# A convolution and two-layer kernel: new homes for w2's parts, block sums in place, another order at the end of layer 1, transposes in rows of four

## The chip, the cores and the metric

One Trainium2 chip, one core. The metric is the device time of one execution in microseconds (us), the median of three runs. Five engines work from queues of their own and wait for each other by semaphores: TensorE (PE; its weight loads PEld), VectorE (DVE), ScalarE (ACT), GpSimd (POOL) and SyncE (SP), which here issues nearly all DMAs.

## The reference

```python
def reference(A_q, A_k, A_v, A_shift_k, A_ssm_k, A_ssm_D, B_x, B_w1, B_b1, B_w2, B_b2, c, w_mod):
    # S = 2048 tokens, D = 640 channels, F = 1728 hidden; all fp32
    x = A_q
    mod = (_silu(c) @ w_mod).reshape(c.shape[0], 6, 1, -1)
    sa, ca, ga, sb, cb, gb = (mod[:, i] for i in range(6))
    h = _layernorm(x, axis=-1) * (1 + ca) + sa
    # _A_ref: 4-tap causal conv of k, times v; a long causal conv per channel (FFT); times h
    x = x + ga * _A_ref(h, A_k, A_v, A_shift_k, A_ssm_k, A_ssm_D)
    h = _layernorm(x, axis=-1) * (1 + cb) + sb
    r = relu(h @ w1 + b1)                 # layer 1
    return x + gb * ((r * r) @ w2 + b2)   # layer 2
```

## The kernel before, in words

**Stages.** The long convolution runs block by block (five blocks of 128 channels) as two-step transforms on TensorE (keys `pa`, `h`, `x`, `qp`, `t`, `y`), with the gate and the first residual (`fin`). The result x1 goes to DRAM; its first two chunks of 256 tokens stay on the chip in the buffers X1a and X1b. Then comes the dense part.

**Layer 1** works in four passes of 512 tokens, two halves T1 and T2 of 256. w1 lies transformed on the chip: six pairs of 128-column blocks (`w16_0` to `w16_5`, in the tiles `TAGS` = S1, S0, S3, S2, S5, S4), and two leftover blocks (12 and 13, the last with 64 columns) in `s6`. Every number is split in a high and a low part (`split`: a copy on ScalarE, a subtraction on VectorE), and each product is three matmuls of 256 columns (`l1`). Passes 1 to 3 use a 2 x 2 block product with seven instead of eight multiplications (`pair`); the seventh is done later (`late`). The leftovers have plain products (`rest`, 25 matmuls a half). Between passes `tokens` loads, normalises and transposes the next chunk (`turned`: two transposes and one evicting, scaling operation for each of five blocks). Hidden tiles are squared and stored in DRAM (`h_d`).

**Layer 2** works in eight chunks of 256 tokens. `w2_pair(p)` loads two raw tiles of w2 into the ring of four staging tiles STG0 to STG3, splits three blocks, forms four sums on GpSimd in a scratch half of `xf`, and splits these as well: six blocks into the tile of the same pair of w1 (`TAGS[p]`), the seventh into `extra2[p]` (two to each of X1a and X1b, the last two in `s6`). `w2_last` puts leftover blocks into `s6`. Hidden tiles come back from DRAM through a ring of eight quarters UP0.0 to UP1.3 (`h_pair`, `h_last`), which the tiles of layer 1 use as well, in the order in which the program asks for them; VectorE forms four sums, and both engines split them into `xp1r`, `ka`, `kz` or `xa`. A chunk has 146 products of 320 columns in seven PSUM banks (`second_layer`), then sums, the gate row, the residual (`xres`, halves of `xf`) and the output.

**Order.** The program records a graph of operations and orders it itself (`order`): a list scheduler that takes, for each engine, the ready operation with the highest priority out of the table `URGE` (due times, in tenths of us, negative), with a cost for each, a model of the DMA queue, and costs `ENTER` and `LEAVE` where TensorE changes its `form`. The order it finds is fixed in the program (`keep_order`); each engine works in it strictly. SyncE has at most six transfers under way (`OUT`): a later one waits for the landing of the sixth before it. All operations are recorded at one line (L407), so rows of the trace are told apart by their tiles.

## Time and profile before

| | us |
|---|---|
| median of three runs (lowest, highest) | 658.59 (658.23, 659.29) |
| the profiled execution | 658.96 |
| its span, first to last instruction | 657.2 |
| TensorE busy in it | 629.6 (96%) |
| VectorE, ScalarE, GpSimd busy | 516.1, 358.1, 226.8 |

```profile
PEclk8999999999999999999999999999999999999999
DMA  9898989999896722563756632145555443553353
```

These two lines of the page cut the span in 40 slices: TensorE's granted clock and the busy share of the 16 DMA engines, both in tenths. The convolution reaches to about 265 us, layer 1 from 280 to 479, layer 2 from 472 to 652. TensorE is the engine that is busy nearly throughout, so a time is read from where it stands still and from what it waited for.

### The profile page before, as it was taken

The page shows a single profiled execution, that of the slowest core. Times are in us where ns is not written, and L with a number is a line of the kernel's source. Part 1 is how long each engine was busy: PE and PEld are TensorE (multiplying, and loading weights), DVE is VectorE, ACT ScalarE, POOL GpSimd, SP SyncE. Part 2 cuts the span into 40 slices and gives each one's busy share as a digit, 9 for nine tenths or more (in the row PEclk, how much of TensorE's full clock was granted, in tenths as well). Part 3 has the DMA queues.
Part 4 walks back from the last instruction along what each step waited for, and adds up shares of the span by engine and source line. Part 5 has one row for each costly group of instructions (what it writes and reads, how often), then busy time and mean ns, then how long its engine had stood idle before and what let it go on. Part 6 is the DMA issues. An engine that isn't in the chain of part 4 may idle for free.

```text
span 657.2 us, 17277 instructions
## 1 busy us (share of the span) xinstructions
PE 629.6 (96%) x7012; PEld 584.4 (89%) x7012; DVE 516.1 (79%) x969; ACT 358.1 (54%) x681; POOL 226.8 (35%) x294
## 2 busy tenths in 40 slices
PE   7999999999999999899999999999989999999996
PEld 7888779878878878499999999999978999999996
DVE  1758848699978666886886787778899989788896
ACT  3554767885866775556585664456463424233321
POOL 1528649768786756311324200235400000000000
PEclk8999999999999999999999999999999999999999
DMA  9898989999896722563756632145555443553353
GB/s 223 217 272 284 267 231 249 208 234 216 229 241 164 142 56 72 156 208 89 213 152 194 193 112 75 56 140 166 159 147 171 151 137 118 166 176 120 114 157 81
DMA packets 143464, 111.00 MB, mean 169 GB/s; under 512 B 50836, under 2 KB 123348, under 8 KB 143384
## 3 DMA queue, kind: packets, MB, share of 16 engines
q1 hardware_dynamic: 141252, 109.28, 60.1%
q8 instruction: 55, 0.90, 0.6%
q10 hardware_dynamic: 2068, 0.61, 0.4%
q14 instruction: 25, 0.20, 0.1%
q0 software_dynamic: 64, 0.01, 0.0%
HBM read 79.99 MB, written 29.88 MB: 167 GB/s over the span
## 4 chain that ended last, share of the span: by engine, by line
PE 49%; DVE 3%; DMA 2%; ACT 1%; issue 1%; DVEq 0%; ACTq 0%
PE ps L407 49%; DMA up<-h_d 2%; DVE up L407 1%; DMA x<-x_d 1%; DVE w L407 0%; DVE ka L407 0%; DVE s L407 0%; DVE xp1r L407 0%; DVE kz L407 0%; ACT w L407 0%; ACT xf L407 0%; DVE xa L407 0%; DVE outs L407 0%; ACT kz L407 0%; ACT xa L407 0%
## 5 line engine op out<-in xcount | busy, mean ns | idle before, releaser
L407 PE MATMUL ps<-a,gb 128*64 128x128 f32 x1260 | 76.8, 275 | 3.3 <-ACT a L407 2.1
L407 PEld LDWEIGHTS ps<-a,gb 128*64 128x64 f32 x1260 | 69.3, 137 | 11.6 <-ACT a L407 5.4
L407 ACT ACTIVATE up<-ps,b1t 128x256 f32<-128x256 f32 (+1 forms) x112 | 50.6, 471 | 48.4 <-PE ps L407 46.4
L407 PE MATMUL ps<-t,w 128*128 128x256 f32 x504 | 72.7, 284 | 0.3 <-DVE up L407 0.3
L407 PEld LDWEIGHTS ps<-cst,p 64*64 64x64 f32 (+1 forms) x1792 | 60.7, 137 | 11.4 <-issue 6.1
L407 PE MATMUL ps<-cst,p 64*64 64x64 f32 (+1 forms) x1792 | 66.7, 247 | 3.9 <-POOL p L407 2.5
L407 PEld LDWEIGHTS ps<-t,w 128*128 128x128 f32 x504 | 64.8, 189 | 0.7 <-DVE up L407 0.5
L407 ACT ACTIVATE a<-ps 128x512 f32<-128x512 f32 x72 | 40.8, 620 | 31.9 <-PE ps L407 31.8
L407 DVE SCALAR_TENSOR_TENSOR up<-up 128x512 f32<-128x512 f32 (+2 forms) x70 | 45.3, 655 | 11.3 <-ACT up L407 10.6
L407 DVE TENSOR_TENSOR up<-up 128x256 f32<-128x256 f32 (+2 forms) x124 | 44.7, 383 | 7.4 <-DMA up<-h_d 5.7
L407 PE MATMUL ps<-xa,w 128*128 128x256 f32 x342 | 49.5, 284 | 0.0
L407 POOL TENSOR_TENSOR wm<-wm,wm 128x640 f32<-128x640 f32 x24 | 38.2, 1591 | 19.7 <-ACT wm L407 19.1
L407 PEld LDWEIGHTS ps<-xa,w 128*128 128x128 f32 x342 | 44.1, 190 | 0.4 <-DVE xa L407 0.2
L407 PE MATMUL ps<-w,xp1r 128*128 128x320 f32 x216 | 40.1, 310 | 1.9 <-ACT up L407 1.1
L407 PE MATMUL ps<-w,xa 128*128 128x320 f32 x216 | 41.1, 309 | 0.0
L407 PE MATMUL ps<-w,kz 128*128 128x320 f32 x216 | 39.9, 310 | 0.6 <-DVE kz L407 0.6
L407 PE MATMUL ps<-w,ka 128*128 128x320 f32 x216 | 40.4, 309 | 0.0
L407 DVE SCALAR_TENSOR_TENSOR kva<-ps,tap,kva 128x511 f32<-128x511 f32 (+2 forms) x48 | 35.8, 747 | 5.5 <-ACT kva L407 3.8
L407 DVE TENSOR_TENSOR up<-ps,up 128x256 f32<-128x256 f32 (+2 forms) x67 | 28.5, 435 | 13.4 <-PE ps L407 8.3
L407 PEld LDWEIGHTS ps<-w,xp1r 128*128 128x128 f32 x216 | 33.7, 188 | 2.6 <-ACT up L407 1.3
L407 PEld LDWEIGHTS ps<-w,kz 128*128 128x128 f32 x216 | 33.6, 188 | 1.0 <-DVE kz L407 1.0
L407 ACT ACTIVATE kz<-up 128x896 fp32r<-128x896 f32 (+2 forms) x24 | 16.8, 699 | 32.1 <-DVE up L407 31.8
(199 smaller groups left out, 1533.4 us busy)
## 6 DMA issues: line engine op xcount, KB each, us to landing
h_d<-up SPq DMA_DIRECT2D x51, 256.0 KB, 2.5
up<-h_d SPq DMA_DIRECT2D x48, 256.0 KB, 3.5
wm<-in_w_mod_dram SPq DMA_DIRECT2D x30, 320.0 KB, 5.2
w1s<-in_B_w_dram SPq DMA_DIRECT2D x25, 320.0 KB, 3.7
p<-in_A_ssm_k_dram SPq DMA_DIRECT2D x20, 256.0 KB, 4.4
p<-kv_d SPq DMA_DIRECT2D x20, 256.0 KB, 4.6
xp<-in_A_q_dram SPq DMA_DIRECT2D x10, 512.0 KB, 8.0
xf<-x_d SPq DMA_DIRECT2D x8, 640.0 KB, 4.1
```

The lines of the kernel that those rows point to most:

```text
L407: fn(*real, **{k: a.real() if isinstance(a, View) else a for k, a in kw.items()})
```

## The change

1. *Homes.* w2's pair 0 goes into X1a, X1b (four of its six blocks) and the last third of `s6` (two); pairs 1 to 5 into the tile of the w1 pair before their own (`TAGS[p - 1]`). The seventh blocks of pairs 0 to 3 go into `xf`'s place, those of pairs 4 and 5 and both leftover blocks into S4. The residual's tiles move from `xf` to the staging tiles.
2. *Sums in place.* The four sums of a pair overwrite the raw tiles.
3. *Last pass of layer 1.* The late product of the last pair and `h_pair(0, 1)` come ahead of the leftovers, `h_pair(0, 2)` between their halves.
4. *Transposes* of chunks 1 to 7 in rows of four (two blocks in one bank), and in the dense part the form of a TensorE operation is its type: going to an fp32 one is charged 0.04 us, to an fp32r one 0.085.
5. *End of layer 2.* Residual loads and stores by 128 tokens; in the last chunk each block is gated and added as soon as it is there, the block (1, 1) in two parts.
6. *`URGE`* is a new table throughout.

```diff
-ENTER = {(64, 128): 0.104}
-LEAVE = {(64, 64): 0.11}
+ENTER = {(64, 128): 0.104, 4: 0.04, 2: 0.085}
+LEAVE = {(64, 64): 0.11, 4: 0.0, 2: 0.0}
...
     def turn(o, x, hold=()):
-        ..., form=(P, P))
+        ..., form=(P, P) if len(g.nodes) <= g.mlp else 4)
...
-    def turned(n, xh, b):
+    def turned(n, xh, bs):
         g.key = ("xt", n)
-        t = psum(f"xtp_{n}_{b}", (P, 2, P), ...)
-        for i in range(2):
-            with g.as_one(0.11):
-                turn(t[:, i], xh[i][:, b * P : (b + 1) * P])
+        t = psum(f"xtp_{n}_{bs[0]}", (P, len(bs), 2, P), ...)
+        turns = [(j, i) for i in range(2) for j in range(len(bs))]
+        for k in range(0, len(turns), len(turns) if n else 1):
+            some = turns[k:] if n else turns[k : k + 1]
+            with g.as_one(0.11 * len(some)):
+                for j, i in some:
+                    turn(t[:, j, i], xh[i][:, bs[j] * P : (bs[j] + 1) * P])
...
-            for b in range(NB):
-                turned(n, xh, b)
+            for bs in ((0, 1), (2, 3), (4,)) if n else ((b,) for b in range(NB)):
+                turned(n, xh, bs)
...
+        if s == NS - 1:
+            late[0]()
+            h_pair(0, 1)
         r = [out_tile(f, s) for f in (NF - 2, NF - 1)]
         rest(s, 1, [v[:, CH:] for v in r])
         if s == NS - 1:
-            h_pair(0, 1)
-        late[0]()
+            h_pair(0, 2)
+        else:
+            late[0]()
...
-        w = W2S[p] = sbuf(f"w2_{p}", (P, 3840), [whole(TAGS[p])], dtype=F32R)...
-        e = W2X[p] = extra2[p].rearrange("p (a f) -> p a f", a=2)
-        temp = xf[:, 1280 * (p % 2) : 1280 * (p % 2) + 1280]
-        t = temp.rearrange("p (k f) -> p k f", k=4)
+        if p:
+            w = sbuf(f"w2_{p}", (P, 3840), [whole(TAGS[p - 1])], dtype=F32R)...
+            u, v, w = w[:, :, 0:2], w[:, :, 2:4], w[:, :, 4:6]
+        else:
+            u, v = (sbuf(f"w2_0{i}", (P, 1280), [whole(f"X1{i}")], dtype=F32R)... for i in "ab")
+            w = s6[:, 2560:3840].rearrange("p (a k f) -> p a k f", a=2, k=2)
...
         split(w[:, 0, 0], w[:, 1, 0], a[:, 0])
-        split(w[:, 0, 1:3], w[:, 1, 1:3], c)
+        split(u[:, 0], u[:, 1], c)
         g.key = ("w2c", p)
-        sub(pool, t[:, 0], a[:, 1], a[:, 0])
-        sub(pool, t[:, 1], c[:, 1], t[:, 0])
-        sub(pool, t[:, 2], c[:, 1], a[:, 1])
-        sub(pool, t[:, 3], c[:, 0], t[:, 1])
+        sub(pool, a[:, 0], a[:, 1], a[:, 0])
+        sub(pool, a[:, 1], c[:, 1], a[:, 1])
+        sub(pool, c[:, 1], c[:, 1], a[:, 0])
+        sub(pool, c[:, 0], c[:, 0], c[:, 1])
...
-                rows = x1_d.buf.real[n * CH : (n + 1) * CH, :].rearrange("(l p) d -> p l d", p=P)
-                sp_dma(x, in_dram(x1_d, rows, n * CH, n * CH + CH, 31), 2560)
+                for i in range(2):
+                    r0 = n * CH + i * P
+                    sp_dma(x[i], in_dram(x1_d, x1_d.buf.real[r0 : r0 + P, :], r0, r0 + P, 31), 2560)
...
-        for i, k in ((1, 0), (0, 0), (0, 1), (1, 1)):
+        def gated(i, k, t, done=True):
             o = slice(320 * k, 320 * k + 320)
-            mul(dve, c[:, i, k], c[:, i, k], row0b[:, o])
-            add(dve, x[:, i, o], x[:, i, o], c[:, i, k])
-            for a in range(2):
-                (act_dma if a else sp_dma)(osrc[a, :, 2 * n + i, o], x[64 * a : 64 * a + 64, i, o], 1280)
+            mul(dve, c[:, i, k], t, row0b[:, o])
+            add(dve, x[i][:, o], x[i][:, o], c[:, i, k])
+            for a in range(2) if done else ():
+                (act_dma if a else sp_dma)(osrc[a, :, 2 * n + i, o], x[i][64 * a : 64 * a + 64, o], 1280)
+
+        gated(1, 0, c[:, 1, 0])
+        add(dve, c[:, 0, 0], ps7[4], u3)
+        gated(0, 0, c[:, 0, 0])
+        add(dve, u2, ps7[5], u2)
+        gated(1, 1, u2, False)
+        add(dve, c[:, 0, 1], ps7[5], u3)
+        gated(0, 1, c[:, 0, 1])
+        gated(1, 1, ps7[3])
...
-        ("hat", 0): [-1183, -2159],
+        ("hat", 0): [2077, -147],
-        ("xs", 0): [-2103, -1773, -2350, -2609, -2958, -2800, -2077, -2273, -2097, -2777],
+        ("xs", 0): [2417, 665, -2623, -2890, -2813, -1174, 2418, -2946, 2420, 667],
-        ("y", 4): [-2576, -2524, -1940, -2560],
+        ("y", 4): [-937, -770, -770, 587],
-        ("lw1", 0): [-2600, -3062],
+        ("lw1", 0): [-1493, -3444],
...
-    xz = [sbuf(f"xz_{i}", (P, 1280), [whole(f"X1{'ab'[i]}")], dtype=F32R) for i in range(2)]
-    extra2 = [xz[p // 2][:, 640 * (p % 2) : ...] for p in range(4)] + [s6[:, 640 * i : 640 * i + 640] for i in range(2)]
+    xe = sbuf("xe", (P, 2560), [WXB], dtype=F32R)
+    extra2 = [xe[:, 640 * i : 640 * i + 640] for i in range(4)]
     for p in range(NP):
+        if p == 4:
+            se = sbuf("se", (P, 3840), [whole(TAGS[5])], dtype=F32R)
+            extra2 += [se[:, 640 * i : 640 * i + 640] for i in range(2)]
         w2_pair(p)
-    w2_last(NF - 2, s6[:, 1280:2560])
-    w2_last(NF - 1, s6[:, 2560:3840])
+    w2_last(NF - 2, se[:, 1280:2560])
+    w2_last(NF - 1, se[:, 2560:3840])
...
-    xres = [xf[:, 1280 * k : 1280 * k + 1280].rearrange("p (i d) -> p i d", i=2) for k in (1, 0)]
+    xres = [[sbuf(f"xr_{k}_{i}", (P, D), [whole(f"STG{2 * k + i}")]) for i in range(2)] for k in range(2)]
```

## Rows read from the trace of the kernel before

**Rows 1.** Sums by stretch: busy us (operations) by engine, clock, DMA share, GB/s.

```profile
0.00:250.00 250.00, 237.25 (x3958) 203.81 (x3960) 182.06 (x318) 163.48 (x313) 160.23 (x230) 0.99 0.86 215
250.00:284.00 34.00, 29.29 (x314) 22.03 (x314) 26.97 (x48) 18.14 (x33) 14.83 (x15) 1.00 0.41 113
284.00:470.00 186.00, 184.62 (x1531) 181.96 (x1531) 146.67 (x308) 111.12 (x240) 46.94 (x46) 1.00 0.46 144
470.00:500.00 30.00, 26.28 (x180) 24.95 (x179) 25.76 (x54) 14.21 (x26) 4.80 (x4) 1.00 0.60 180
500.00:652.00 152.00, 152.00 (x1038) 151.68 (x1036) 133.04 (x240) 51.17 (x71) 0.00 (x0) 1.00 0.45 138
```

**Rows 2.** Order of time, TensorE: start, us, operation xcount [idle before <-releaser].

```profile
478.29 0.71 PE L407 MATMUL ps<-w,xp1r 128*128 128x320 f32 x3 [0.80 <-DVE up L407]
...
480.42 0.71 PE L407 MATMUL ps<-w,xp1r 128*128 128x320 f32 x3 [1.07 <-ACT up L407]
...
485.10 1.74 PE L407 MATMUL ps<-w,kz 128*128 128x320 f32 x10 [0.57 <-DVE kz L407]
...
499.05 0.41 PE L407 MATMUL ps<-s,kz 128*128 128x320 f32 x1 [1.23 <-DVE kz L407]
```

**Rows 3.** Order of time, VectorE, where layer 2 begins.

```profile
476.02 1.89 DVE L407 TENSOR_TENSOR up<-up 128x128 f32<-128x128 f32 x4 [2.26 <-DMA up<-h_d]
477.83 0.41 DVE L407 TENSOR_TENSOR up<-ps,up 64x256 f32<-64x256 f32 x1
...
497.53 0.89 DVE L407 TENSOR_TENSOR up<-up 128x256 f32<-128x256 f32 x2 [1.05 <-DMA up<-h_d]
498.44 0.55 DVE L407 TENSOR_TENSOR kz<-up,kz 64x384 fp32r<-64x384 f32 x1
```

**Rows 4.** Order of time, VectorE, its last three operations.

```profile
652.16 0.49 DVE L407 TENSOR_TENSOR outs<-ps,outs 128x320 f32<-128x320 f32 x1
652.68 0.49 DVE L407 TENSOR_TENSOR outs<-outs,gbrow 128x320 f32<-128x320 f32 x1
653.21 0.49 DVE L407 TENSOR_TENSOR xf<-xf,outs 128x320 f32<-128x320 f32 x1
```

**Rows 5.** Order of time, TensorE, transposes (ident,x) among products of layer 1.

```profile
395.26 0.27 PE L407 MATMUL ps<-ident,x 128*128 128x128 f32 x1
395.28 0.60 PE L407 MATMUL ps<-xa,w 128*128 128x256 f32 x3
395.72 0.53 PE L407 MATMUL ps<-kz,w 128*128 128x256 f32 x3
396.08 0.52 PE L407 MATMUL ps<-xa,kz 128*128 128x256 f32 x3
...
408.60 0.60 PE L407 MATMUL ps<-ident,x 128*128 128x128 f32 x4
408.96 0.95 PE L407 MATMUL ps<-t,w 128*128 128x256 f32 x6
409.75 0.53 PE L407 MATMUL ps<-ident,x 128*128 128x128 f32 x3
```

**Rows 6.** Order of time, TensorE and then VectorE, where the convolution ends.

```profile
266.92 1.50 PE L407 MATMUL ps<-ident,q 128*128 128x128 f32 x12 [1.81 <-DVE q L407]
...
277.17 0.93 DVE L407 TENSOR_TENSOR w<-w1s,w 128x640 fp32r<-128x640 f32 x1
278.16 0.99 DVE L407 TENSOR_SCALAR xf<-ps,cbs 128x256 f32<-128x256 f32 x2
```

**Rows 7.** Order of time, GpSimd, two sums of w2's blocks.

```profile
472.28 2.22 POOL L407 TENSOR_TENSOR xf<-w2s,w2s 128x320 f32<-128x320 f32 x1 [9.35 <-DMA w2s<-in_B_w_dram]
474.46 0.87 POOL L407 TENSOR_TENSOR xf<-w2s 128x320 f32<-128x320 f32 x1
```

**Rows 8.** Layer 2: SyncE's waits (us in total, times, longest); its transfers (KB each, us to landing).

```profile
SPq L618 <- DMA out_dram<-xf: 19.3, 6, 3.7
...
xf<-x_d SPq DMA_DIRECT2D x7, 640.0 KB, 4.1
```

More of the change, by code (lines that the diff above doesn't have):

```diff
@@ L681, in mm @@
         ins = [x for x in (a, b) if isinstance(x, View)]
-        g.add("PE", 0.0, (nc.tensor.matmul, "matmul", (o, a, b), dict(start=start, stop=stop, **({"skip_group_check": True} if more else {}))), [o], ins, entries=n, hold=hold, form=(a.p[1] - a.p[0] if isinstance(a, View) else a.shape[0], o.p[1] - o.p[0]))
+        g.add("PE", 0.0, (nc.tensor.matmul, "matmul", (o, a, b), dict(start=start, stop=stop, **({"skip_group_check": True} if more else {}))), [o], ins, entries=n, hold=hold, form=(a.p[1] - a.p[0] if isinstance(a, View) else a.shape[0], o.p[1] - o.p[0]) if len(g.nodes) <= g.mlp else n)
     def turn(o, x, hold=()):
-        g.add("PE", 0.0, (nc.tensor.transpose, "transpose", (o, x, ident), {}), [o], [x] if isinstance(x, View) else [], entries=2, hold=hold, form=(P, P))
+        g.add("PE", 0.0, (nc.tensor.transpose, "transpose", (o, x, ident), {}), [o], [x] if isinstance(x, View) else [], entries=2, hold=hold, form=(P, P) if len(g.nodes) <= g.mlp else 4)
     def copy(eng, o, i, hold=()):
@@ L1522, in l2, with rest2 @@
                 mm(acc, h[a], w[y], first and i == 0, last and i == 2)
+    def rest2(n, ps7, i):
+        k, o = {2: (1, 0), 4: (0, 0), 5: (0, 1), 3: (2, 1)}[i]
+        g.key = ("l2", n)
+        a, c = HS[n, "a"], HS[n, "c"]
+        wa, wc = W2S[NF - 2], W2S[NF - 1]
+        o = slice(320 * o, 320 * o + 320)
+        l2(ps7[i], parts(a, k), (wa[:, 0, o], wa[:, 1, o]), False, False)
+        with g.as_one(0.294):
+            mm(ps7[i], c[:, k], wc[:, 0, o], False, False)
+            mm(ps7[i], cone[n % 2][:, k], wc[:, 1, o], False, False)
     def second_layer(n):
@@ L1528, in second_layer @@
         for p in range(NP):
-            if n == 0 and p + 2 < NP:
+            if n == 0 and 0 < p and p + 2 < NP:
                 h_pair(0, p + 2)
@@ new lines, in ssm_mlp_kernel @@
+        ("h", 3): [-1650, -1932, -1912, -1941, -1635, -1982, -1830, -1874, -1946, -2062, -1893, -2088, -1664, -1905,
+            -1536, -1979],
+        ("h", 4): [-2363, -2396, -2195, -2416, -2436, -2288, -459, -2287, -2054, -1960, -2502, -2144, -2492, -2510,
+            -2065, -1950],
+        ("hat", 0): [2077, -147],
+        ("hat", 1): [-2764, -3073],
+        ("hat", 2): [-2895, -2820],
+        ("hat", 3): [-3432, -2566],
+        ("hat", 4): [-2234, -2234],
+        ("hat", 5): [-2360, -2274],
@@ new lines, in ssm_mlp_kernel @@
+        ("mul", 4): [-2426, -2315, -2426, -2456, -2512, -2158, -2475, -2097, -2331, -2511, -2504, -2503, -2503, -2576,
+            1546, 1259],
+        ("one", 0): [-4261, -4758, -4820, -4274, -4503, -4204],
+        ("out", 0): [-4087, -4801, -5167, -3753, -5132, -5099, -1316, -4223, -5482, -5526, -4965, -5172, -5446, -4631,
+            -5208, -5311],
+        ("out", 1): [-5638, -5177, -5371, -5536, -5347, -5037, -5345, -5486, -5253, -5586, -5462, -5483, -5986, -5687,
+            -5654, -5654],
```

243 lines of the change are left out of this document (111 added, 132 removed), and 655 rows, old and new, of the table URGE.

## The prediction

> **What bounds the kernel now.** I read the sums by stretch first [rows 1]. TensorE is busy for 152.00 of the 152.00 us of layer 2 behind 500 us and for 184.62 of 186.00 us of layer 1; no edit here takes products away, so these two stretches can't give more than 1.4 us together. Its idle time lies in three places: 12.75 us (250.00 - 237.25) in the first 250 us, 4.71 us where the convolution ends and layer 1 begins (250 to 284 us), and 3.72 us where layer 1 ends and layer 2 begins (470 to 500 us). After the last matmul come VectorE's last adds and the last writes, 5.2 us.
>
> Then the order of time in the third place [rows 2]: four gaps, 0.80, 1.07, 0.57 and 1.23 us, together 3.67. For what stands behind them I read VectorE's queue there [rows 3]. At 476.02 it begins work on a hidden tile whose load from DRAM has just landed, after 2.26 us of idling; the bias add that frees a PSUM bank stands behind it and runs at 477.83, and TensorE goes on at 478.29. At 497.53 the same again: 1.05 us for a load that chunk 1 needs, and behind it at 498.44 a small split that chunk 0 needs at once; TensorE waits 1.23 us. So these gaps aren't a lack of VectorE time (25.76 of 30.00 us busy [rows 1]); they are an order in which work that is not yet fed stands ahead of work that is awaited.
>
> **The change, part by part.** The time comes out of the order, so each part is priced by the idle time that it can remove.
>
> *Homes of w2's parts, and the leftover tiles last in pass 3.* No instruction is added: each pair keeps five splits (ScalarE copy, VectorE subtraction) and four GpSimd subtractions. What moves is when they may run. Pair 0 goes into the x1 buffers and a part of `s6` that layer 1 doesn't use; pairs 1 to 5 take the tile of the pair of w1 before their own, so each can be written one pair of layer 1 earlier. `xf` becomes the home of four of the "extra" blocks, and the tile of w1's last pair that of the rest. With pair 5 finished before the leftover products, that tile falls free while two times 25 products are still to run, and the second pair of chunk 0's hidden tiles is asked for ahead of both leftover blocks and the third between them, instead of the second between and the third behind. The work that stood at VectorE's head at 476.02 is thereby earlier in the ring of eight quarters, and its load can be issued earlier. The leftovers' own evictions, two per token half, are now the last ones, so the wait for a bank can recur there: I keep one of 0.7 us, near the 0.57 and 0.80 us of [rows 2]. Term: 3.7 - 0.7 = 3.0 us less. Bounds: all 3.7 us gone, or one wait of the largest size added to all that is there (+1.2).
>
> *Block sums in place.* As many GpSimd operations as before; 0.87 us each when alone and 2.22 us at worst [rows 7]. New are waits: the first sum may start only when both halves of the split of `a[:, 0]` have read it, and the raw tiles are held until the last split, not until the last sum. Behind GpSimd's head stands only the next sum; on SyncE's queue the load of the raw tiles two pairs on. The cover is the pair that is one home ahead. Off the path: 0; bounds 0 and +2.2, one slow sum on it. The operation of 2.22 us ran beside VectorE, the one of 0.87 us hardly [rows 7]. The Trainium skill says of this ("SBUF — State Buffer", section "SBUF: two separate sides") that GpSimd and a VectorE operation with two SBUF inputs exclude each other on a shared port pair for the whole instruction. By that rule in-place sums, which now alternate with VectorE's subtractions, would run nearer to 2.22 than to 0.87 us; four per pair stay behind the products all the same, and the sum is left as it is.
>
> *Transposes in rows of four.* Chunks 1 to 7 of layer 1 have 70 transposes, in 30 runs of one to four now and in 21 rows afterwards. A lone one: from 395.26 to 395.72 us one transpose and three products took 0.46 us; three products alone (395.72 to 396.08) 0.36; the transpose cost 0.10. In a row of four: 408.60 to 409.75 is 1.15 us for four transposes and six products; less 6 x 0.12 leaves 0.43, or 0.108 each [rows 5]. So a row saves nothing that can be seen, though the planner's table now charges 0.04 + 0.085 us for going there and back. Taken: 0. Bound: 9 fewer runs x 0.125 = 1.1 us less; nothing on the other side, since a bank held by two blocks is awaited only by the next chunk's work.
>
> *The last chunk's end.* Before, three VectorE operations follow the last product in line, from 652.16 to 653.70 us, each some 0.52 from start to start [rows 4]. Now each gated block is added as soon as it is there, and for the last one the part without `ps7[3]` has been multiplied and added already: a multiply out of PSUM and an add are left. Term: 0.5 us less. It costs one more multiply and add earlier, beside TensorE. Bounds: 1.0 us more where these two push the last pair back; 0.5 less.
>
> *Residual and output in halves.* Per chunk one more load, two more stores, on SyncE, which has at most six transfers under way. Layer 2 has no TensorE idling to show for SyncE's waits so far [rows 1, 8]. Taken: 0; the other end is the third rival.
>
> *All due times drawn anew.* This is the widest part. Where the convolution ends there is one chain (transform, gate, statistics, normalise, transpose, first products), and other work stands in it on VectorE: a split of w1 of 0.93 us at 277.17 runs ahead of the two evictions (278.16) that the first products of layer 1 wait for, and TensorE waits 1.81 us at 266.92 for a copy that VectorE was late with [rows 6]. In the new table the keys that feed that chain (`hat` 0, the first of `xs` 0, `y` 4) come far forward, and w1's loads come earlier, so its splits can run before the chain. Of 4.71 us I take a third, 1.5. Bounds: 3.7 less (1 us is left), 1.5 more (three splits like that of 0.93 us in the way instead of one, partly covered). For the first 250 us, where the due times of the first blocks hardly change, 0, with 1 us either way.
>
> **Sum.** 3.0 + 0.5 + 1.5 = 5.0 us less. The profiled execution took 658.96 us in all, with a span of 657.2 and 1.8 around it; it would become 654.0. The median of the runs, 658.59, is 0.4 below that execution, so 653.6 us.
>
> **The rivals.**
> First, *both seams close*: boundary 3.7, start 3.7, end 0.5: 7.9 us less, 650.7 us. For it speaks that most of the waits there are waits in a queue and not for a busy engine; against it, that the start is a chain with fixed latencies, of which the rows show one split of 0.93 us and one late copy only.
> Second, *the waits move*: the loads of the hidden tiles land later than planned as they did at 476 and 497 us, and VectorE again stands for them with an eviction behind; the start is as before. Only the end is left: 658.1 us. For it: the order is fixed beforehand, and in both head waits [rows 3] VectorE had come to its work before the load had landed. Against it: the loads are now asked for ahead of the leftovers.
> Third, on the other side, *SyncE's queue in layer 2*. It already waited 19.3 us in six waits for landings of the output, up to 3.7 us each, and a 640 KB residual load takes 4.1 us to land [rows 8]. With 14 transfers a chunk instead of 11 on one queue with six under way, the loads of the next chunk's hidden tiles stand behind stores that wait for VectorE. From the point where they land later than the previous chunk's last product, each of the seven chunk starts shows a gap such as the one of 1.23 us [rows 2]: 8.6 us, less the 5.0 above: 662.2 us. Against it: not one gap in 152 us of layer 2 so far. On halves: the 640 KB load took 4.1 us [rows 8]; the Trainium skill ("DMA: Bandwidth & Descriptors", section "Bandwidth") wants transfers in pieces of a megabyte or more, since each pays a fixed part. By that rule two halves would cost more than the whole and this rival gains; no run here shows a half.
>
> **How the numbers follow.** The forecast has 0.55, both seams 0.15, the waits that move 0.17, SyncE's queue 0.13. About 0.2%, 1.3 us, is what a measurement of this kernel can tell from no change. Faster by more than that: 0.70; within it: 0.17; slower: 0.13. The forecast's own bounds are 1.5 to 2.5 us either way. The range reaches from 649.5 (the first rival with the 1.1 us of the transposes) to 659.2 (the second with 1 us lost in the first 250); outside lie the third and a little on both sides.
>
> **What would show it.** Right: 470 to 500 us (some 2 us earlier by then) with under 1 us of TensorE idling, no eviction behind a wait for a load on VectorE, two VectorE operations behind the last product. The start: under 3.5 us of idling between the last transform and steady layer 1. Transposes: the same 0.11 us each in rows. Wrong: gaps of TensorE at the starts of layer 2's chunks, released by splits that waited for loads; or idling in the first 250 us above 13.8 us; or the four gaps again at other places with the same sum.

## The result, and the profile after

The changed kernel takes 662.52 us (median of 13 runs, 658.28 to 665.11) against 660.16 for the kernel before on the same chip (13 runs): a ratio of 1.0045, 95% interval 1.0024 to 1.0065. It is slower by about 0.45%, where 653.6 us and a gain were predicted; 662.5 also lies above the range. The profiled execution took 664.42 us with a span of 662.6, and the granted clock of TensorE averaged 0.992 in it (before: 0.997).

Each run lists its span and its mean granted clock. (1 - clock) x span is the time that half speed took away, if TensorE had work all the while. Over the 82 runs of the kernel before that were made beside the experiments (on three chips) it is 2.0 us on average and the rest of the time 657.5; over 25 runs of the changed kernel (13 here, 12 in the first experiment) 4.0 and 658.5, with standard errors of 0.2 to 0.4. So of 3.0 us some 2.0 go with the clock and 1.0 with work and waits.

Sums by stretch, as in [rows 1] (busy us (operations) of PE, PEld, DVE, ACT, POOL, then clock, DMA share, GB/s):

```profile
0.00:250.00 250.00, 232.40 (x3892) 201.45 (x3894) 174.69 (x314) 161.74 (x311) 154.97 (x226) 0.99 0.83 212
250.00:284.00 34.00, 30.75 (x367) 24.05 (x364) 26.62 (x47) 17.36 (x32) 15.30 (x17) 1.00 0.33 94
284.00:470.00 186.00, 184.43 (x1520) 181.36 (x1519) 146.05 (x307) 108.84 (x240) 46.24 (x48) 1.00 0.49 150
470.00:500.00 30.00, 26.79 (x168) 25.29 (x168) 26.66 (x55) 16.11 (x28) 5.79 (x5) 0.89 0.51 162
500.00:652.00 152.00, 151.88 (x1035) 151.56 (x1034) 130.40 (x237) 51.66 (x73) 0.00 (x0) 1.00 0.49 141
```

From 470 to 500 us TensorE still stands still for 3.21 us (30.00 - 26.79; 3.72 before), and its clock there is 0.89 instead of 1.00. Behind 500 us nothing has changed. TensorE there, in order of time, answering [rows 2]:

```profile
473.94 0.97 PE L407 MATMUL ps<-xa,w 128*128 128x256 f32 x6 [0.38 <-ACT up L407]
...
486.64 0.41 PE L407 MATMUL ps<-w,kz 128*128 128x320 f32 x1 [0.23 <-DVE kz L407]
...
491.55 0.58 PE L407 MATMUL ps<-xe,xa 128*128 128x320 f32 x2 [1.86 <-ACT xa L407]
492.68 0.63 PE L407 MATMUL ps<-xe,xa 128*128 128x320 f32 x1 [0.55 <-DVE xa L407]
493.11 5.00 PE L407 MATMUL ps<-w,xa 128*128 128x320 f32 x18
```

The four gaps of before are gone, but with one more of 0.19 us these add up to 3.21: the largest is now a wait for the split of a hidden tile of chunk 0 (`xa`). The 18 products behind it take 5.00 us; at full speed the same 18 take 2.79 (shown below). VectorE and ScalarE ahead of that wait, answering [rows 3]:

```profile
478.56 1.15 DVE L407 TENSOR_TENSOR up<-up 128x128 f32<-128x128 f32 x4 [1.30 <-DMA up<-h_d]
...
481.50 0.46 DVE L407 TENSOR_TENSOR up<-up 128x128 f32<-128x128 f32 x1 [0.87 <-DMA up<-h_d]
...
491.53 1.09 DVE L407 TENSOR_TENSOR xa<-up,xa 128x896 fp32r<-128x896 f32 x1
```

```profile
488.81 0.74 ACT L407 ACTIVATE se<-w2s 128x640 fp32r<-128x640 f32 x1 [3.35 <-DMA w2s<-in_B_w_dram]
490.55 0.95 ACT L407 ACTIVATE xa<-up 128x896 fp32r<-128x896 f32 x1 [1.00 <-DVE up L407]
```

VectorE still idles for loads of hidden tiles, 1.30 and 0.87 us. An eviction still stands behind the first of these loads (480.23 us), but TensorE no longer waits for it. From 481.96 to 495 us VectorE has no wait of 0.15 us or more. The profile of before shows the same once it is read this way: from 476.02 to 496.4 us, between the two waits for loads of [rows 3], VectorE has none either. ScalarE waited 1.00 us for VectorE before it could copy `xa`, so VectorE is late, not ScalarE.

Three milestones split the time. Columns: first product of layer 1; from it to layer 1's last; from there to layer 2's last; from there to the end; where the granted clock was at half speed (us from the start), without the stretch at the very end, which all have.

| profile | first | layer 1 | to last of layer 2 | end | half speed |
|---|---|---|---|---|---|
| before | 279.80 | 199.28 | 172.74 | 5.38 | 11.2-14.6 |
| before, a second time | 278.94 | 199.35 | 172.66 | 5.38 | 480.5-483.9 |
| after | 281.36 | 200.50 | 175.85 | 4.94 | 44.8-48.2, 492.0-498.8 |
| after_again | 278.23 | 200.48 | 174.59 | 4.95 | 489.5-492.9 |
| after_rows_one_engine | 279.54 | 199.70 | 173.86 | 4.95 | none |
| after_vector_when_idle | 283.35 | 200.43 | 173.39 | 4.95 | 134.1-137.5, 178.5-181.9, 270.7-274.1 |
| before_end_alone | 278.34 | 199.10 | 172.78 | 5.09 | none |

So layer 1 has become 1.2 us longer, the way from there through layer 2 0.7 and 1.1 us longer in the two profiles without half speed in it (173.39 and 173.86 against 172.7), the end 0.44 us shorter; the start of layer 1 is unchanged where no stretch at half speed lies ahead of it.

That last point is a balance. In the first 250 us TensorE stands still for 17.60 us (250.00 - 232.40; 17.27 in after_again) instead of 12.75, which is above the 13.8 us that the prediction names as a sign of being wrong. From 250 us to the first product of layer 1 it stands still for 3.15 us instead of 4.63. And for the same 4238 operations up to there it is busy for 257.8 to 259.2 us in three profiles of the new order without half speed ahead of layer 1, against 261.6 and 261.7 in two of before's.

### The profile page after: what moved, and what is told of

Same layout as the page of the kernel before. It is cut to its first block, busy times and chain, and to the rows that moved or that the text cites. A ratio compares the mean times of both kernels' runs of the same rounds, so it can differ in the third digit from the quotient of the medians.

```text
span 662.6 us, 17296 instructions
## 1 busy us (share of the span) xinstructions
PE 632.3 (95%) x7012; PEld 589.5 (89%) x7012; DVE 511.1 (77%) x970; ACT 355.7 (54%) x681; POOL 222.3 (34%) x294
## 4 chain that ended last, share of the span: by engine, by line
PE 76%; DVE 7%; DMA 6%; ACT 5%; issue 4%; SPq 1%; ACTq 0%; POOL 0%; DVEq 0%; POOLq 0%
PE ps L407 76%; DVE up L407 2%; DMA xp<-in_A_q_dram 1%; SPq L618 1%; DMA p<-in_A_ssm_k_dram 1%; DMA p<-kv_d 1%; DMA up<-h_d 1%; DMA d<-in_A_ssm_D_dram 1%; DVE kva L407 1%; DVE kacc L407 1%; DMA kv_d<-kacc 1%; DVE w L407 1%; ACT a L407 1%; DVE wxa L407 1%; ACT q L407 1%
## 5 line engine op out<-in xcount | busy, mean ns | idle before, releaser
L407 DVE SCALAR_TENSOR_TENSOR up<-up 128x512 f32<-128x512 f32 (+3 forms) x70 | 45.9, 670 | 8.2 <-ACT up L407 7.7
L407 ACT ACTIVATE xp1r<-up 128x896 fp32r<-128x896 f32 (+1 forms) x16 | 13.4, 844 | 43.1 <-DVE up L407 30.0
L407 PEld LDWEIGHTS ps<-w,xa 128*128 128x128 f32 x216 | 36.0, 200 | 0.0
L407 DVE TENSOR_TENSOR outs<-ps,outs 128x320 f32<-128x320 f32 x55 | 26.4, 488 | 11.0 <-PE ps L407 9.0
L407 PE MATMUL ps<-kz,w 128*128 128x256 f32 x216 | 34.6, 286 | 0.1
```

The costliest lines, as they stand in the source:

```text
L407: fn(*real, **{k: a.real() if isinstance(a, View) else a for k, a in kw.items()})
```

## The experiments

Where a kernel is built from an order, `ORDER` and `PLACES` are after's own order and buffers, written out, so that nothing moves but what the diff names; `MOVES` puts one step of an engine ahead of another. "The seam" is the end of layer 1.

**after_again.** Is the wait an accident of one execution?

```diff
-    g.emit(g.order())
+    g.emit(moved_up(g, g.order(), []))   # nothing moved
```

> The changed kernel once more, its planned order written down unchanged. Theory A (orders): the loss of about 3 us lies in fixed places of the new order, so a second profile shows them again: a wait of 1.5 us or more of TensorE for xa, the third hidden pair of chunk 0, near 490 us (1.86 and 0.55 us in the first profile), 1.0 us or more later at the first layer-1 product than before (279.80 us), and a layer-1 stretch about 1.2 us longer. Theory B (the clock by itself): the first profile's granted clock of 0.992 came by chance in that execution; a second profile shows the low stretches (44.81 to 48.22 and 491.96 to 498.78 us) elsewhere or not at all, and where they are absent the kernel takes 658 to 660 us. Ratio to the kernel before: 1.003 to 1.006 under both.

662.32 us (12 runs), ratio 1.0038 [1.0018, 1.0059]. The wait for `xa` is there again, 1.85 and 0.57 us, with half speed right behind it, and layer 1 is as long as in after (200.48 us). The half speed at 44.8 us is not there, nor the later first product of layer 1 that theory A expected (278.23 us). The wait has a fixed place, the clock hasn't.

**after_xa_early.** Four steps that `xa` needs go ahead of steps that are needed later.

```diff
+MOVES = [
+    (('DVE', ('hc', 0), 14), ('DVE', ('w2s', 5), 3)),   # its two sums ahead of a split of w2
+    (('DVE', ('hc', 0), 15), ('DVE', ('w2s', 5), 3)),
+    (('ACT', ('hs', 0), 6), ('ACT', ('w2s', 6), 2)),    # high part ahead of a leftover block's copy
+    (('DVE', ('hs', 0), 7), ('DVE', ('ev', 3), 61)),    # low part ahead of a square
+]
```

> The changed kernel with three steps moved at the end of layer 1 and nothing else: on VectorE the last two sums of the third hidden pair (xa) ahead of a split of w2, and its low part ahead of a squared hidden tile; on ScalarE its high part ahead of the copy that waited 3.35 us for the load of w2's leftover block. Theory A: the waits of 1.86 and 0.55 us go, and the low clock of 491.96 to 498.78 us, which cost 2.2 us on 18 products (4.80 us for what takes 2.65 at full clock), goes with them: 2 to 4.7 us less than the changed kernel, ratio to the kernel before 0.998 to 1.001. Theory B: at most the 2.4 us of waits go (ratio 1.001), the low clock stays. Rival to both: the next load or split is late instead, and TensorE waits as long one pair further on (ratio 1.0045).

663.53 us (9 runs), ratio 1.005 [1.0025, 1.0075]. TensorE in order of time:

```profile
490.39 0.41 PE L407 MATMUL ps<-xe,xa 128*128 128x320 f32 x1 [0.33 <-DVE xa L407]
495.36 0.79 PE L407 MATMUL ps<-se,xp1r 128*128 128x320 f32 x2 [1.92 <-ACT xp1r L407]
```

The wait for `xa` is gone and stands before the next hidden pair, at the same size and with half speed behind it. All waits of the seam: 3.77 us.

**after_first_stage_of_before.** The convolution in before's order, the dense part in after's.

> The changed kernel, but its convolution (the first 277 us) in the order and with the buffers that the kernel before had there; layer 1 and layer 2 in the changed kernel's order. Theory A: the convolution's new order costs 1 to 1.6 us (first layer-1 product at 281.36 us instead of 279.80), so this is 1 to 1.6 us faster than the changed kernel, ratio 1.002 to 1.003, with the first product of layer 1 near 280 us and no low clock at 45 us. Theory B: the first product is as late as in the changed kernel, within 0.5 us, or the low clock at 45 us comes as well; ratio 1.0045.

678.28 us, ratio 1.028. The splice opened one wait of 6.34 us in layer 1 (295.75 us, for an eviction on VectorE), layer 1 took 212.6 us, and 20 us at half speed came with it. So it can't price the convolution's term. It shows two things beside it: with before's order there TensorE has no pause for its own instructions ahead of layer 1 (more on these below), and half speed came in that order too (185.1 to 191.9 us).

**before_two_orders.** The other way round: before, with the new last chunk's end and with the awaited steps of its own seam (and of its own start) moved ahead of the unfed ones.

```diff
+    (('DVE', ('ev', 3), 59), ('DVE', ('hc', 0), 4)),     # eviction ahead of the sums at 476.02
+    (('DVE', ('hs', 0), 3), ('DVE', ('w2s', 6), 1)),
+    (('ACT', ('ev', 3), 55), ('ACT', ('w2s', 5), 2)),
+    (('DVE', ('hs', 0), 14), ('DVE', ('hc', 1), 0)),     # the split behind 497.53
+    (('DVE', ('qpc', 4), 7), ('DVE', ('w1s', 4), 3)),    # start of layer 1
...
```

> The kernel before with the new end of the last chunk (the last block's other part multiplied and added ahead of time, two VectorE steps behind the last product instead of three) and ten steps moved forward, nothing else: at the end of layer 1 an eviction ahead of the hidden sums that wait for their load, the low part of the first two hidden pairs ahead of splits and squares, an eviction on ScalarE ahead of two copies of w2, the small split of kz ahead of chunk 1's sums; where layer 1 begins a copy of q and the first two transposes' evictions ahead of a split of w1. Theory A (the gaps are an order, not a lack of engine time): 2 to 3 us of the 3.7 at the end of layer 1, 0.5 to 1.5 where it begins and 0.5 at the end go: ratio 0.993 to 0.995. Rival: the waits move to the next step in the queues and only the 0.5 us at the end stays: ratio 0.999.

661.2 us (12 runs), ratio 1.0022 [0.9998, 1.0046]. TensorE and ScalarE:

```profile
482.79 1.17 PE L407 MATMUL ps<-w,xp1r 128*128 128x320 f32 x3 [2.69 <-ACT up L407]
```

```profile
480.67 0.74 ACT L407 ACTIVATE s<-w2s 128x640 fp32r<-128x640 f32 x1 [2.63 <-DMA w2s<-in_B_w_dram]
481.31 0.93 ACT L407 ACTIVATE ka<-up 128x896 fp32r<-128x896 f32 x1
482.26 0.47 ACT L407 ACTIVATE up<-ps,b1t 128x256 f32<-128x256 f32 x1
```

TensorE's waits behind the two loads of [rows 3] are gone, and one of 2.69 us on ScalarE takes their place: an eviction stands behind a copy that waited 2.63 us for its w2 load and began at 480.67 us (477.20 in the profile of before). With four smaller ones behind it (0.46, 0.80, 0.17, 0.53) the waits add up to 4.65 us. So these moves brought nothing of the 2 to 3 us that theory A expected, and the ratio is above the rival's 0.999 as well.

**after_fill.** Fifteen products into a spare bank stand in the wait for `xa`, to see whether half speed there comes from TensorE standing still.

```diff
+                if (n, p, i) == (0, 2, 3):
+                    fill(g.nodes[-1], 12)   # and 3 behind the second of the next three
```

> The changed kernel in its own order with fifteen products more, whose sum nobody reads: twelve ahead of the third hidden pair's first product (xa, where TensorE waited 1.86 us), three ahead of the product with its low part (0.55 us); 15 x 0.133 = 2.0 us of work in 2.4 us of waiting, into the PSUM bank that is free then. Theory C (a single wait of 1.85 us or more is what lowers the granted clock behind it; the waits themselves cost as much as the four of before): no low clock between 480 and 505 us, the wait's 2.4 us all but gone as idle time, and 1 to 2 us less than the changed kernel in the mean of the runs, ratio to the kernel before 1.000 to 1.0025. Rival (the clock falls there by itself, or for another reason than TensorE's idling): a low stretch of 3.4 us or more in 485 to 505 us as before, ratio 1.004.

661.53 us (9 runs, mean 663.0), ratio 1.006 [1.0034, 1.0086]. In its profile no half speed at the seam, but two stretches ahead of layer 1 (227.5, 268.5 us), and over its runs the time lost to the clock is 3.8 us (standard error 0.6), as in after. As a cure it does nothing. One profile without half speed at this place shows no cause either: after_rows_one_engine and after_vector_when_idle have none there without any fill, right behind the wait.

**after_rows_one_engine.** Layer 1's 1.2 us. A row of transposes fills one bank with two blocks, and after evicts one of them on VectorE, the other on ScalarE. What ended VectorE's idle time ahead of its own half of these evictions (290 to 470 us; us, times), in the profile of after; in that of before the line for ScalarE is 0.7 us in three waits:

```profile
its engine sat idle before it (us, times) until:
  ACT xf L407: 4.0, 7
```

```profile
373.87 0.66 PE L407 MATMUL ps<-ident,x 128*128 128x128 f32 x4 [0.61 <-ACT xf L407]
...
374.72 0.60 PE L407 MATMUL ps<-ident,x 128*128 128x128 f32 x4
375.07 0.60 PE L407 MATMUL ps<-t,w 128*128 128x256 f32 x3
375.51 0.52 PE L407 MATMUL ps<-xa,s 128*128 128x256 f32 x3
```

VectorE waits seven times for the semaphore that ScalarE raises behind its half (the second fence is TensorE: its row at 373.87 waits 0.61 us for a bank).

```diff
-            if b % 2:
+            if (b // 2 if n else b) % 2:   # both blocks of a row on the same engine
                 act.activation(o, t2, AF.Identity, scale=c1, bias=c0)
```

> The changed kernel, but both blocks of a row of transposes are evicted by one engine (rows by turns VectorE and ScalarE) instead of one block by each. Theory D (layer 1 is 1.2 us longer because two engines take a shared bank one after the other: VectorE waited 4.0 us in 7 waits for ScalarE's eviction of the same row, never in the kernel before): these waits go, TensorE's 0.61 us wait for a bank at the row near 371 us and 0.31 us for an eviction near 411 us shrink or go, and layer 1 from its first to its last product takes 199.3 to 199.9 us instead of 200.5. Rival (the row's bank itself is what is held too long, whoever empties it: the two evictions of one engine take 1.1 us, as long as the two in turn): waits of the same size at the rows, 200.3 us or more.

660.58 us (10 runs), ratio 1.0025 [1.0003, 1.0047]; layer 1 takes 199.70 us in this profile, 199.61 in a second one, 199.11 and 199.08 in two kernels that contain the edit and moved steps besides, against 200.1 to 200.5 in six profiles without it (a seventh, after_xa_early, has 201.9 with waits of 0.58 and 0.34 us more in it). VectorE's waits for ScalarE's `xf` are gone. So the shared bank is shown to cost layer 1 some 0.8 us.

It is not shown to be what made layer 1 longer than before. Between its first and last product TensorE stands still for 2.06 us in after (2.37 and 2.17 in after_again and after_vector_when_idle), no more than in before (2.25, and 2.59 and 2.38 in the two other profiles of its order); with the edit it is 1.3 to 1.6. What grew is TensorE's busy time for the same 1624 operations: 198.1 to 198.4 us against 196.7 to 197.0, and still 197.6 to 198.2 with the edit. Where that 1.2 us comes from is open. The waits of the seam are 3.57 us with the edit, so some of the gain goes into them. A second profile of this kernel (after_rows_and_seam) gave 668.55 us, layer 1 199.61, the same wait (1.85 and 0.57) and 20 us at half speed in four places:

> The kernel with each row of transposes evicted by one engine, once more, for a second profile: layer 1 from first to last product 199.7 us within 0.3, no wait of VectorE for ScalarE's eviction of the same row; the same wait of 1.86 and 0.57 us near the end of layer 1, with or without a low clock behind it.

**xa_early_less_vector.** Is VectorE short of time? after_xa_early without most of the low parts of two blocks of w2, 1.45 us of VectorE (the outputs lack these parts).

```diff
-            split(u[:, 0], u[:, 1], c)
+            copy(act, u[:, 0], c)
+            sub(dve, u[:, 1, :, 0:1], c[:, :, 0:1], u[:, 0, :, 0:1])   # pair 5 only; w likewise
```

> The kernel with xa's steps moved forward, less 1.45 us of VectorE's work at the end of layer 1: the low parts of two w2 pieces (128x640 each, 0.75 and 0.70 us) are left out, their products read the high part twice, so their share of the sum is missing. Theory E (VectorE is short of time between 481 and 495 us, where it had no idle moment): the waits at the end of layer 1, 3.8 us in all in the kernel with xa's steps moved, lose 1.2 to 2 us, mostly of the 1.92 us at the fourth pair. Rival (the hidden tiles' loads, issued only when the pair two before has been split, set the pace): the wait for the fourth pair stays within 0.4 us.

658.48 us (one run). The wait before the pair is still 1.88 and 0.56 us, and all waits of the seam fall from 3.77 to 2.82, by 0.95 us. As written beforehand that speaks for the rival: the wait for the fourth pair stays, and the drop is below the 1.2 to 2 us of theory E. For theory E speaks that TensorE comes to that pair 18.76 us after its first product of layer 2 instead of 20.61; but VectorE also waited less for the hidden tiles' loads here (1.02 us instead of 2.63). This run doesn't decide between the two. With it ran **before_again**, a second profile of before (658.11 us):

> The kernel before once more, for a second profile. Under every theory the same four waits at the end of layer 1 (0.80, 1.07, 0.57, 1.23 us, each within 0.3) and layer 1 at 199.3 us. Theory C: no low clock behind them, since none of them alone reaches 1.85 us; if a low stretch does show between 478 and 505 us, theory C is wrong in its size.

Its waits at the seam are 1.12, 1.27 and 0.72 us, so three of the four are not within 0.3 us of the first profile. Half speed stands behind the second: before has it there too, at times, and theory C, which wanted a wait of 1.85 us, is wrong in its size.

**rows_and_hidden_first, rows_hidden_loads_later.** Two more orders, both on the kernel of after_rows_one_engine: all steps of hidden pairs 3 and 4 ahead of splits that are needed later; then also two loads of w1 behind two stores near 200 us.

```diff
+    (('DVE', ('hc', 0), 14), ('DVE', ('w2s', 5), 3)),   # ... to 19, and the low parts
+    (('ACT', ('hs', 0), 8), ('ACT', ('hs', 0), 12)),
+    (('SP', ('lh2', 0), 7), ('SP', ('lh1', 3), 13)),
...
+    (('SP', ('fin', 2), 7), ('SP', ('lw1', 3), 0)),     # second kernel only
+    (('SP', ('fin', 2), 9), ('SP', ('lw1', 3), 0)),
```

> The kernel with each row of transposes evicted by one engine, and at the end of layer 1 all of chunk 0's hidden pairs 3 and 4 ahead of w2's splits and of the leftover tile's steps on VectorE and ScalarE, the load of the fifth pair ahead of a store on the queue. Theory F (the order of VectorE's queue places the waits: the last sum of the fourth pair stood behind a small split, the third pair's behind a w2 split): the waits at 485 to 497 us shrink from 2.4 us to 1.3 or less, each under 0.8 us, so the low clock behind them goes too; ratio to the kernel before 0.996 to 1.000. Rival (the loads set the pace, 3.5 us after the pair two before has been split): a wait of 1.5 us or more stays at the third, fourth or fifth pair; ratio 1.002 to 1.003.

> The same, and in the convolution two loads of w1 (320 KB each, issued near 200 us) put behind two stores of x on the queue, as they stood in the kernel before. Theory G (TensorE's waits that the profile calls issue, 1.2 to 2.3 us near 200 to 204 us in the changed kernel and none there before, come from its instructions' own transfers standing behind w1's loads: DMA share 0.75 to 0.91 there): that wait shrinks to 0.6 us or less and the first product of layer 1 comes 0.6 to 1.5 us earlier; ratio 0.994 to 0.998. Rival (the wait has another cause, or moves to the next place where the queues are full): issue waits of 3 us or more in all between 170 and 230 us as before, ratio as without it.

663.04 us (12 runs), ratio 1.0048 [1.0023, 1.0074], and 661.19 (12), 1.0025 [1.0008, 1.0042]. The wait is now 2.10 us and stands before the leftover pair, at 500.04 and 494.88 us. All waits of the seam are 4.87 and 3.02 us. The two loads of w1 were moved for another reason: in the convolution of the new order TensorE pauses without waiting for anything that the profile shows ("issue") at three places, in after:

```profile
178.48 0.94 PE L407 MATMUL ps<-gi,wxb 64*128 64x128 f32 x13 [1.35 <-issue]
...
204.14 0.59 PE L407 MATMUL ps<-we,cst 128*64 128x512 f32 x1 [1.23 <-issue]
...
228.98 0.68 PE L407 MATMUL ps<-cst,p 64*64 64x64 f32 x27 [1.66 <-issue]
```

Before has none above 0.84 us in three profiles. The sums (us, times, longest) ahead of layer 1, of after and then of before:

```profile
PE ps L407 <- issue: 4.6, 4, 1.7
PE ps L407 <- issue: 1.0, 2, 0.7
```

With the loads moved the three are 1.26, 1.78 and 1.56: moving these loads didn't help.

**after_vector_when_idle, after_vector_when_busy.** What sets the sum of the waits? The same extra time goes to VectorE twice: before its idling for the loads, and behind it.

```diff
+AGAIN = [('DVE', ('w2s', 3), 9, 4)]   # when idle: this split four times instead of once
+AGAIN = [('DVE', ('w2s', 6), 1, 3)]   # when busy: this one three times
```

> After, with the split of one hidden tile repeated three more times on VectorE (0.40 us each, 1.2 us in all) where VectorE is about to stand idle for the next hidden tile's load, near 476.8 us. Nothing is left out. Theory (VectorE's time behind those loads sets the sum of TensorE's waits at the end of layer 1; what it idles ahead of them is lost either way): the sum of the waits there stays at 3.2 to 3.4 us, +-0.4. Rival (VectorE is short over the whole end of layer 1): the sum grows by 1.2 us, to 4.4 to 4.6. Rival (the loads or ScalarE set the pace): it stays, here and in after_vector_when_busy.

> After, with the split of a later hidden tile's low part repeated two more times on VectorE (0.7 us each, 1.4 us in all) in the stretch where VectorE has no idle moment, near 484.3 us. Nothing is left out. Theory (VectorE's time behind the loads sets the sum): the sum of TensorE's waits at the end of layer 1 grows by 1.2 to 1.5 us, to 4.4 to 4.9. Rival (VectorE short over the whole end): the same growth, and in after_vector_when_idle too. Rival (the loads or ScalarE set the pace): it stays at 3.2 to 3.4, +-0.4.

Both took 663.88 us (one run each). VectorE, then TensorE, of after_vector_when_idle:

```profile
478.51 2.06 DVE L407 TENSOR_TENSOR xe<-w2s,xe 128x320 fp32r<-128x320 f32 x4
...
482.92 0.42 DVE L407 TENSOR_TENSOR up<-up 128x128 f32<-128x128 f32 x1 [0.36 <-DMA up<-h_d]
...
496.80 1.56 DVE L407 TENSOR_TENSOR xp1r<-up,xp1r 128x896 fp32r<-128x896 f32 x2 [0.35 <-ACT xp1r L407]
```

```profile
476.84 0.60 PE L407 MATMUL ps<-w_0b,xp1r 128*128 128x320 f32 x3
...
488.71 2.36 PE L407 MATMUL ps<-w,kz 128*128 128x320 f32 x15
492.93 0.56 PE L407 MATMUL ps<-xe,xa 128*128 128x320 f32 x2 [1.86 <-ACT xa L407]
...
494.31 2.79 PE L407 MATMUL ps<-w,xa 128*128 128x320 f32 x18
```

And of after_vector_when_busy:

```profile
484.06 2.94 DVE L407 TENSOR_TENSOR se<-w2s,se 128x640 fp32r<-128x640 f32 x4
...
496.83 1.56 DVE L407 TENSOR_TENSOR xp1r<-up,xp1r 128x896 fp32r<-128x896 f32 x2 [0.35 <-ACT xp1r L407]
```

```profile
475.26 0.60 PE L407 MATMUL ps<-w_0b,xp1r 128*128 128x320 f32 x3
...
488.06 0.41 PE L407 MATMUL ps<-w,kz 128*128 128x320 f32 x1 [1.91 <-DVE kz L407]
...
488.75 3.89 PE L407 MATMUL ps<-w,kz 128*128 128x320 f32 x15
492.96 0.56 PE L407 MATMUL ps<-xe,xa 128*128 128x320 f32 x2 [0.32 <-ACT xa L407]
```

Counted from the first product of layer 2 (475.11 in after, 476.84, 475.26), VectorE comes to the last split shown after 20.31 us (495.42) in after, 19.96 when idle, 21.57 when busy. So 1.58 us more work in front of the loads cost nothing (VectorE's waits for them fell from 2.17 to 0.36 us), and 1.72 us more behind them cost 1.3 to 1.6. The sums of TensorE's waits, by which the theories were to be told apart, don't say so: they are 3.36 and 3.73 us, the second below its 4.4 to 4.9 and within what the rival (loads or ScalarE) allowed. There 15 products took 3.89 us instead of 2.36, at half speed from 488.9 to 492.3, and the wait behind them is 1.54 us shorter for it: with the slow products the sum is 5.26. VectorE's arrival speaks for the first theory, but it was chosen as the measure after the runs, from one profile each.

**before_end_alone.** The one term that held, by itself on before (the block done in two parts is (0, 0) here).

```diff
+        gated(0, 0, u3, False)
+        add(dve, c[:, 1, 1], ps7[3], u2)
+        gated(1, 1, c[:, 1, 1])
+        gated(0, 0, ps7[4])
```

> Before, with the last chunk's end of after alone (the last sums and stores in halves in the new order). The step of the sum it prices: -0.5 us, bounds +1.0 to -0.5. By the profiles of the changed kernel's runs (last product of layer 2 to the end 4.94 to 4.95 us, before 5.38) it should take 0.3 to 0.45 us off, a ratio of 0.9993 to 0.9995. Rival: the gain in the profile's tail is not seen in the time, ratio 1.000 or above.

659.27 us (10 runs) against 659.63 (13): ratio 0.9989 [0.9972, 1.0005]. Last product to end 5.09 us instead of 5.38. The profile shows a gain of 0.29 us; the times agree with it and can't tell it from nothing.

## Why the prediction was wrong, step by step

**Homes and leftovers last: -3.0 predicted, about 0 measured.** This is the step that failed. The waits of the seam are 3.67, 3.11 and 3.62 us in the three profiles with before's order there, 3.21 and 3.38 in the two of after. The failing sentence is "these gaps aren't a lack of VectorE time (25.76 of 30.00 us busy [rows 1]); they are an order". The share of a stretch was the wrong number: VectorE's idle time lies ahead of the hidden tiles' loads, and behind them it has none of 0.15 us or more for 13 us in after and for 20 us in before. Idle time before the loads can't be spent on what comes after them; 1.58 us of extra work placed there was free, and 1.72 us behind cost 1.3 to 1.6. All five orders tried kept 3.0 to 4.9 us of waits and moved the largest to the next operand (`xa`, `xp1r`, the leftover pair, ScalarE's eviction in before). That no move removed the waits is shown; that VectorE's time behind the loads sets their sum is argued from its rows and from one profile each, and xa_early_less_vector doesn't confirm it. The second rival, "the waits move", described what happened, with its mechanism (the loads of hidden tiles, VectorE standing for them); it got 0.17. The last line of the prediction, "the four gaps again at other places with the same sum", is what happened. If the account holds, a cure has to bring the loads forward or take work off VectorE behind them; no run shows one.

**What no term had: the clock.** The forecast carried the clock of one profile of before (0.997) over to after. Each of the stretches of 3.4 us at half speed (1.2 GHz) in the table is worth up to 1.7 us. At the seam half speed follows the waits of the seam in after, after_again and after_xa_early, but not in after_rows_one_engine or after_vector_when_idle, which have the same wait of 1.86 us; before_again has it behind waits of 1.1 and 1.3 us. In the convolution eight of eleven profiles with the new order have at least one, all but one of these between 134 and 277 us; the three profiles of before's own order have one in all, at 11 us, and the one of after_first_stage_of_before, with before's order there, has one at 185. So the new order loses more time at half speed, over the runs by 2.0 us; why, by its waits or by its pauses for instructions, is not shown. Nor does each stretch cost its 1.7 us: in after_vector_when_busy the slow products took the place of a wait.

**Transposes in rows: 0 predicted, with "nothing on the other side"; the shared bank costs some 0.8 us.** In the row shown the price of a transpose is as predicted: from 374.72 to 375.51 us four transposes and three products take 0.79 us; less 0.36 for the three products [rows 5] that leaves 0.108 each. Wrong was the reason given for the bound: a bank held by two blocks is awaited not by the next chunk's work only, but by the other engine that evicts from it. With both evictions on one engine layer 1 is 199.1 to 199.7 us, against 199.1 to 199.4 in before; but that is the balance of shorter waits and 1.2 us more of TensorE's busy time, whose cause is open. The Trainium skill ("PSUM — Partial Sum Buffer", section "PSUM bank collisions raise a hardware error") says that two engines may not be in one bank on the same partitions at a time, two readers included, and that software has to keep them apart. The seven waits for ScalarE's semaphore are what that costs this program. It speaks against this part of the change, and the prediction left it out.

**In-place sums: 0 predicted, 0 to 2.2 kept as bounds.** They have moved to another place and run beside VectorE, as in after:

```profile
488.02 0.88 POOL L407 TENSOR_TENSOR w2s<-w2s,w2s 128x320 f32<-128x320 f32 x1 [6.21 <-DVE w L407]
488.98 1.19 POOL L407 TENSOR_TENSOR w2s<-w2s 128x320 f32<-128x320 f32 x1
```

```profile
486.50 0.61 DVE L407 TENSOR_TENSOR up<-up 128x128 f32<-128x128 f32 x2
...
488.21 1.24 DVE L407 SCALAR_TENSOR_TENSOR up<-up 64x512 f32<-64x512 f32 x1
489.38 1.14 DVE L407 TENSOR_TENSOR up<-up 128x128 f32<-128x128 f32 x2
```

Beside these sums two of VectorE's additions take 1.14 us instead of the 0.61 just before, and a square 1.24 instead of the 0.68 that the same shape takes in before (478.89 us): about 1.1 us, just ahead of the wait for `xa`. In after_xa_early VectorE's low part of `xa` (488.62 us) falls there and takes 1.72 us instead of 1.09, and the second sum 1.60. The Trainium skill's statement that a GpSimd operation and a VectorE operation with two SBUF inputs exclude each other ("SBUF — State Buffer", section "SBUF: two separate sides") agrees with these numbers. The prediction weighed it for GpSimd's sums alone, and left out the other side, that VectorE is held up as well, in the very stretch in which it has no time to spare. Before has some of it too (its four additions at 476.02 take 1.89 us [rows 3], the same four 1.15 in after), and how much of the seam it is, no run took apart.

**New due times: -1.5 at the start and 0 in the first 250 us predicted, together about 0 measured.** The second part was wrong. Where the convolution ends, TensorE's idle time fell by 1.5 us, the size forecast (4.63 to 3.15 us from 250 us to layer 1). But in the first 250 us it grew from 12.75 to 17.60, far over the 1 us either way; 3.6 us of that are the pauses for instructions. That layer 1 begins no later all the same is owed to a busy time 2 to 4 us shorter, which no term foresaw. The chain at the start is the same, with its waits elsewhere:

```profile
267.09 0.94 PE L407 MATMUL ps<-gi,wxa 64*128 64x128 f32 x12 [0.77 <-POOL wxa L407]
269.20 1.50 PE L407 MATMUL ps<-ident,q 128*128 128x128 f32 x12 [1.17 <-DVE q L407]
...
280.32 0.73 PE L407 MATMUL ps<-ident,up 128*128 128x128 f32 x4 [0.34 <-DVE xf L407]
281.36 8.10 PE L407 MATMUL ps<-t,w 128*128 128x256 f32 x63 [0.31 <-ACT t L407]
```

In place of the wait of 1.81 us of [rows 6] stands one of 1.17, with 0.77 and 0.34 at other links of the chain. Without half speed ahead of it layer 1 begins at 277.5 to 279.5 us in the new order (three profiles) and at 278.3 to 278.9 in that of before (two). The pauses for instructions and the clock did not stand in the sum.

**The last chunk's end: -0.5 predicted, -0.44 measured by the profiles.** Right, by the mechanism named: behind the last product a multiply out of PSUM and an add are left (answering [rows 4]).

```profile
658.05 0.49 DVE L407 TENSOR_TENSOR outs<-ps,gbrow 128x320 f32<-128x320 f32 x1
658.58 0.49 DVE L407 TENSOR_TENSOR xr<-xr,outs 128x320 f32<-128x320 f32 x1
```

**Residual and output in halves: 0 predicted, 0 measured.** SyncE's waits for landings of the output fell, in ten waits instead of six (answering [rows 8]):

```profile
SPq L618 <- DMA out_dram<-xr: 12.6, 10, 2.6
```

Layer 2 has 151.88 us of TensorE in 152.00. The third rival, which was to end on the slow side, didn't come; the slow side came from elsewhere.

**The sum as measured.** Layer 1 +1.2, from there through layer 2 +0.7 without half speed, the end -0.44: +1.5 by the profiles; +1.0 by the runs once the clock is taken out, and 2.0 for the clock, with standard errors of 0.3 and 0.4. The two agree within these errors. Of the +0.7, 0.5 is busy time as in layer 1 (170.3 us against 169.8 in before), and its cause is open too. Of the 8.9 us between 653.6 and 662.5 us, 1.6 lie in the base: the forecast started from 658.59, the median of three runs, and 13 runs gave 660.16.

## What to carry to other kernels

A busy share over a stretch doesn't show whether an engine has time: split the stretch at the last load that the engine waits for, and count only what is idle behind it. Where two engines are to take turns on one bank, ask who waits for the first of them. Price a new order of an almost gapless kernel by the sum of its waits over several profiles, by the busy time of the engine that bounds it, and by the granted clock of all runs: here each wait that was moved named the next, and a start that looked unchanged hid two changes that cancelled.

## What the runs showed of the hardware

- Two engines that evict two halves of one PSUM bank did not run side by side in this program: VectorE waited seven times, 4.0 us in all, for the semaphore behind ScalarE's half, though they read different columns. What they would do without that semaphore no run shows.
- The granted clock fell to 0.50 for 3.4 us or more at the seam in ten of sixteen profiles, in or behind waits of 1.1 to 2.7 us, and in three others it didn't behind waits of 1.9 to 2.1 us. A single profile is no measure of it.
- TensorE paused 0.7 to 2.4 us with no wait that the profile shows ("issue") at three places of the convolution, in all eleven profiles of the new order; in the three of before's own order no such pause is over 0.84 us. The cause is open: loads moved away from one of the places changed nothing.
- A VectorE operation with two SBUF inputs took 1.72 us instead of 1.09 beside two sums of GpSimd (after_xa_early), and the second sum took 1.60 us instead of 0.87 [rows 7].
